# Recurrent attention with two expert layers on one core: attention's side steps reordered, GpSimd's queue in layer 1, unused products in the last chunks

## The chip, the cores and the metric

One core of one Trainium2 chip runs the kernel. The metric is the device time of one execution in microseconds; the kernel before was timed three times, and the median counts. The profile is of one further execution of the same program.

## The reference, cut to what matters

Three parts follow each other on 4 sequences of 768 tokens, with 8 heads of 48 channels:

```python
for t in range(768):                       # attention: a state of 48x48 per head
    cur = einsum('bhd,bhe->bhde', u * k_t, v_t)
    y_t = einsum('bhd,bhde->bhe', r_t, state + cur)
    state = w_t * state + einsum('bhd,bhe->bhde', k_t, v_t)
x = y reshaped to 3072 tokens x 384
...
e = argmax(x @ w_gate + modality_bias[modality_id])      # layer 1: one expert of 8 for a token
x = softmax weight * (relu(x @ w1[e]) @ w2[e])
...
top2 of x @ w_gate + log1p(exp(x @ w_noise)) * noise     # layer 2: two experts of 8 for a token
out = sum over the two: softmax weight * (relu(x @ w1[e]) @ w2[e])
```

The hidden width of an expert is 1024. Products of the expert layers are made as three f16 products (high times high, high times low, low times high), so each weight is converted into a high part by ScalarE and a low part by VectorE.

## The kernel before, in words

**Attention** (`attention`, L306) works in 24 chunks of 128 tokens, six to a sequence. The loop over `i` from -4 to 23 is a software pipeline whose order is written out by hand: in iteration `i` TensorE gets, in this order, `scores(i + 1)` (L422), `logits(i - 2)` (L221, the gate of layer 1), `outputs(i)` (`ps` L452, `py` L457 and L459), `turn(i - 1)` (L497), `keys_back(i + 1)` (L439) and the transposes of `k` and `r` of chunk `i + 3` and of `w` of chunk `i + 4` (L377). VectorE gets `products(i + 2)` (KT L402, RT L404), the two scans `decays_a` and `decays_b` (L386, L396), `diag` (L410), `state` (L469, L470) and `sums` (L479). ScalarE copies out of PSUM (`am` L427, `kt` L441, `xt` L499, `S` L476) and squares the rows (`norm`, L485). GpSimd masks `am` (L432) and makes `av` and `q` (L414, L369, L370).

At the end of an iteration stand the extra steps. `todo` holds those of layer 1's routing: after each sequence `route1a` in four steps `x` = 0 to 3 (logits out of PSUM, first maximum and exponential, `ranks` on TensorE at L250 to L254, row indices), one step an iteration, and `route1c`, which scatters the rows by index to the table R1 in DRAM (L537, on GpSimd's queue). `extra` holds what prepares the first visit of layer 1: the choice of its expert from counts (`first_a` to `first_d`, `counts` at L262), the gather of its weights (GW), the steps of their conversion (EC: `square` L794, `total` L207, `scales`, `split` with the high part at L812 and the low part at L815), the gather of its rows and their conversion (EX: L864, L226, L227, and a transposing DMA on SyncE's queue, L903). The constants FI, GW, N0, EC and EX say in which iteration each comes. A step that returns a function (the low part) has it called at once.

**Layer 1** makes seven visits of up to 448 rows of one expert (`Jobs.visit`, `Jobs.run`). A visit is eight blocks of the first product (L834, nine products each) and then the second product in columns (L849). Work for the neighbouring visits hangs in numbered slots, one after each block or half column: `turn_back` (L1112) and the gate of layer 2 for the visit before (L221), the fetch of the next visit's rows (`begin` at slot FE, its steps at slots XS), the scatter to table R2 of the visit two before (eight scatters, L1084, slots SCS), weights for later visits. The routing of layer 2 (`route2`, L1005) is a generator of some fifty VectorE steps, drawn four at a time by `tick` in the first eight slots; what is left is run at the end of the visit. Its last five operations are on GpSimd (L1076 to L1080), and with them ends what a scatter needs.

**Layer 2** runs 16 parts, eight experts with 512 and then 320 rows.

All DMAs of one queue start in the order of the program, and GpSimd's queue carries gathers, scatters and its own arithmetic in one order. The tiles of `pm` (logits, ranks, counts) share one PSUM bank.

Of the kernel before, what the change touches and what calls it, by code (L numbers as in the profile page):

```python
# [8 lines left out]
F32 = mybir.dt.float32  # L9
# [3 lines left out]
OP = mybir.AluOpType  # L13
# [5 lines left out]
P = 128  # L19
E = 8  # L20
# [3 lines left out]
NT = TOK // P  # L24
# [34 lines left out]
OE = 1  # L59
WI = -4  # L60
GI = (1, 2, 5, 8)
FI = 9
GW = (11, 12, 13, 16)
N0 = 15
EC = (15, 16, 17, 18, 18, 19, 20, 21, 22, 23, 23)
S1 = 3
EX = (19, 20, 20, 21, 21, 22)
FE = 1
CH = (6, 6, 6, 0)
TB = (0, 4)  # L70
LG = 2
XS = (1, 5, 6, 7, 8, 9)
XS1 = (5, 8, 9, 10, 11, 12)
SC1 = (0, 1, 1, 2, 3, 4, 5, 6)
SCS = (3, 4, 5, 6, 7, 8, 9, 10)
WS = (4, 5, 6, 7), (11, 12, 13, 14)


def bc(ap, shape):
    return ap.to_broadcast(shape)  # L80
# [3 lines left out]
def kernel(  # L84
# [163 lines left out]
    def ranks(x, m16, n, pr):  # L248

        nc.tensor.matmul(pr, tri, m16, start=True, stop=False)  # L250
        for c in range(n - 1):
            nc.tensor.matmul(pr[:, c + 1:, :], ones, bc(m16[:, c:c + 1, :], [P, n - 1 - c, E]),
                             start=False, stop=False)
        nc.tensor.matmul(pr, ones, bc(seen[x][:, None, :], [P, n, E]), start=False, stop=True)  # L254
        with nc.allow_low_precision(reason="counts up to 48 are exact"):
            sums = small.tile([P, E], F16, name="sums")
            nc.vector.tensor_reduce(sums, m16.rearrange("p c e -> p e c"), axis=AX, op=OP.add)
            nc.vector.tensor_tensor(seen[x], seen[x], sums, op=OP.add)
# [47 lines left out]
    def attention(extra):  # L306

        with ExitStack() as st:
# [173 lines left out]
            def norm(t):  # L482
                b, c = divmod(t, NC)
                sq = keep.tile([P, D], F16, name="sq")
                nc.scalar.activation(sq, row(t)[:, 0:META].bitcast(F32), AF.Square,  # L485
                                     accum_out=row(t)[:, META:ROW].bitcast(F32)[:, SS:SS + 1])
                if c == NC - 1:
                    meta = X[b % 2][:, :, META:ROW].bitcast(F32)
                    nc.gpsimd.tensor_copy(meta[:, :, 0], tok_all[:, b * NC:(b + 1) * NC])
                    nc.gpsimd.tensor_copy(meta[:, :, 2:2 + E], noise_sb[:, b * NC:(b + 1) * NC, :])  # L490

            def turn(t, pt=None):

                pt = ps_a.tile([P, HP, P], F32, name="pA") if pt is None else pt
                x = row(t)[:, 0:META].bitcast(F32)
                for i in range(NI):
                    nc.tensor.transpose(pt[:, i, :], x[:, i * P:(i + 1) * P], ident)  # L497
                XT[t] = keep.tile([P, NI, P], F32, name="xt", bufs=2)
                nc.scalar.copy(XT[t], pt[:, 0:NI, :])  # L499
# [7 lines left out]
            def route1a(b, x):  # L507

                sh = [P, NC, E]
                if x == 0:  # L510
                    R = RB[b] = {n: small.tile(s, d, name=f"r1{n}") for n, s, d in (
                        ("lg", sh, F32), ("ex", sh, F32), ("oh16", sh, F16), ("sm", [P, NC], F32),
                        ("ri", sh, F32), ("rf", [P, NC], F32), ("idx", [P, NC], I32))}
                    nc.vector.tensor_tensor(R["lg"], pl[b % 2], bias_all[:, b * NC:(b + 1) * NC, :], op=OP.add)
                    R["mx"], R["oh"], R["fm"] = first_max(R["lg"], NC, "r1")
                    R["fm"][0]()
                    return
                R = RB[b]
                if x == 1:
                    for f in R["fm"][1:]:  # L520
                        f()
                    nc.vector.tensor_tensor(R["lg"], R["lg"], bc(R["mx"][:, :, None], sh), op=OP.subtract)
                    nc.gpsimd.tensor_copy(R["oh16"], R["oh"])
                    nc.scalar.activation(R["ex"], R["lg"], AF.Exp)
                elif x == 2:
                    ranks(0, R["oh16"], NC, pr[b % 2])
                    nc.vector.tensor_reduce(R["sm"], R["ex"], axis=AX, op=OP.add)
                    nc.vector.tensor_scalar(R["sm"], R["sm"], 1e-9, None, op0=OP.add)
                    nc.vector.reciprocal(X[b % 2][:, :, META:ROW].bitcast(F32)[:, :, 1], R["sm"])
                else:  # L530
                    nc.vector.tensor_tensor(R["ri"], pr[b % 2], bc(erow[:, None, :], sh), op=OP.add)
                    nc.vector.tensor_tensor(R["ri"], R["ri"], R["oh"], op=OP.mult)
                    nc.vector.tensor_reduce(R["rf"], R["ri"], axis=AX, op=OP.add)
                    nc.vector.tensor_copy(R["idx"], R["rf"])
# [20 lines left out]
            for t in range(2, NL):  # L555
                load(t)

            def at(f, t):
                if 0 <= t < NT:
                    f(t)  # L560

            for i in range(-4, NT):
                for n, g in enumerate(data):
                    if i >= GI[n]:
                        next(g, None)
                if i >= 0:
                    at(scores, i + 1)
                at(norm, i - 1)
                at(products, i + 2)
                at(decays_a, i + 3)  # L570
                if i >= 0:
                    at(scores_out, i + 1)
                    at(masks, i + 1)
                at(logits, i - LG)
                at(decays_inv, i + 3)
                at(decays_b, i + 3)
                if i == -2:
                    scores(0)
                    scores_out(0)
                    masks(0)  # L580
                    if OE:
                        keys_back(0)
                o = {-1: 0, 0: -1}.get(i, i) if OE else i
                at(outputs, o)
                at(diag, i + 2)
                at(state, o)
                at(turn, i - 1)
                if i >= KB and (i >= 0 or not OE):
                    at(keys_back, i + 1)
                at(state_out, o)  # L590
                at(diag_v, i + 2)
                at(sums, o)
                for n, t in (("kr", i + 3), ("w", i + 4)):
                    at(lambda t: transposes(t, n), t)
                if 0 <= i < KB:
                    keys_back(i + 1)
                if i == WI:
                    warm(WARM[1])
                at(loads_q, i + 3)
                if i >= -2 and i + NL + 2 <= NT:  # L600
                    load(i + NL + 2)
                if i >= 0:
                    nc.sync.dma_start(out[i * P:(i + 1) * P, :], zt)
                for at_i, f, b, x in todo:
                    if at_i == i:
                        f(b, x)
                for f in extra.get(i, []):
                    f()

            last = {"rows": [lambda: norm(NT - 1)], "turn": lambda pt: turn(NT - 1, pt),  # L610
                    "logits": [lambda t=t: logits(t) for t in range(NT - LG, NT)],
                    "route": [], "scatter": []}
# [297 lines left out]
    class Jobs:  # L910
# [94 lines left out]
        def route2(self, xg, q, group="R2"):  # L1005
# [3 lines left out]
            t = lambda shape, n, dt=F32: vp.tile([P] + shape, dt, name=n)  # L1009
            R.row = X[q % 2][:, 0:NH, :]  # L1010
            R.inv = t([NH], "inv2")
            nc.gpsimd.memset(R.inv[VP // 32 * 32:P, :], 0.0)
            meta = xg[:, 0:NH, META:ROW].bitcast(F32)
            rm = R.row[:, :, META:ROW].bitcast(F32)

# [17 lines left out]
            def steps():  # L1033
# [39 lines left out]
                    yield dv.tensor_reduce(zi, z, axis=AX, op=OP.add)  # L1073
                for x in range(2):
                    yield dv.tensor_tensor(idx[:, x, :], zz[x][1], big, op=OP.add)
                nc.gpsimd.memset(rm, 0.0)  # L1076
                nc.gpsimd.tensor_copy(rm[:, :, 0], tok)
                nc.gpsimd.tensor_tensor(wa, o1, bc(d2[:, :, 0:1], sh), op=OP.mult)
                nc.gpsimd.tensor_tensor(tmp, o2, bc(d2[:, :, 1:2], sh), op=OP.mult)
                nc.gpsimd.tensor_tensor(rm[:, :, 1:1 + E], wa, tmp, op=OP.add)  # L1080
                R.idx = idx

            def scatter_one(h, x):
# [88 lines left out]
    def layers():  # L1172
# [5 lines left out]
        def add(hooks, s, f):  # L1178
            hooks.setdefault(s, []).append(f)
# [75 lines left out]
        def once(f):  # L1255
            f = f()
            if callable(f):
                f()

        def some(n):  # L1260
            for _ in range(n):
                once(steps0.pop(0))

        xsteps = []

        def begin(j, sidx):
# [6 lines left out]
                     (EC[0], lambda: steps0.extend(conv0()))):  # L1273
            add(extra, i, f)
        for i in EC:
            add(extra, i, lambda: some(1))
        for i in GW:
            add(extra, i, lambda: wsteps.pop(0)())
        for i in EX:
            add(extra, i, lambda: once(xsteps.pop(0)))  # L1280

        with tc.manual_schedule():
            last = attention(extra)
        with ExitStack() as st:
# [91 lines left out]
            with tc.manual_schedule():  # L1376
# [12 lines left out]
                for j in range(VISITS):  # L1389
                    hooks = {}  # L1390
                    q = max(0, j - EV + 1)
                    if j == 0:
# [11 lines left out]
                        add(hooks, S1 + 2, lambda: begin(1, early["sidx1"]))  # L1404
                        for s in XS1:
                            add(hooks, s, lambda: xsteps.pop(0)())
                        spread(hooks, steps0, (0, 1, 2, 3, 4, 5, 6))
                    else:
                        if j == 1:
                            for x, s in enumerate(T_PLAN):  # L1410
# [181 lines left out]
```

## Time and profile before

| | us |
|---|---|
| timed runs, median (lowest to highest) | 882.61 (881.57 to 887.2) |
| the profiled execution | 883.38 |
| span of its profile | 881.6 |
| TensorE busy in the span | 841.1 |
| mean granted TensorE clock | 0.954 of full |
| attention, up to the first block of layer 1 | about 211 |
| the seven visits of layer 1 | about 260 |

In the rows below a time is counted from the span's start. The chain of waits is followed back from the last instruction. A granted clock of 1.00 is TensorE's upper level (2.4 GHz) and 0.50 its lower one (1.2 GHz); figures between are a stretch with both.

### The profile page before, as it was taken

To read this page: it belongs to the slowest core of one execution; us is meant where nothing else is said; L and a number is where in the kernel's file an instruction comes from. 1 tells how busy PE (TensorE), PEld (TensorE's weight loads), DVE (VectorE), ACT (ScalarE), POOL (GpSimd) and SP (SyncE) were. 2 spreads that over 40 slices of the span, in tenths; PEclk is the share of its full clock that TensorE was granted. 3 is DMA by queue.
4 is the path that set the end of the run, shared out by engine and by line. 5 is a ranking of instruction groups with operands and counts; after the bars stand their busy time and mean duration, and the time that the engine had idled before them with its cause. 6 is when DMAs were issued, how large, how long until landed. Compare 5 with 4: busy or idle time off the path is not lost.

```text
span 881.6 us, 16060 instructions
## 1 busy us (share of the span) xinstructions
PE 841.1 (95%) x6161; PEld 633.1 (72%) x6161; DVE 464.3 (53%) x1244; ACT 435.0 (49%) x819; POOL 360.5 (41%) x404
## 2 busy tenths in 40 slices
PE   7999999989999989899999999999999999999993
PEld 6989999888576566565666678667686766768672
DVE  7979779873674466458666624333332423333220
ACT  2545346554354475567776426445444634534220
POOL 7957697942333161540424642232122223212222
PEclk9999799966999989999999999999999999999997
DMA  9986487423454231743574384864756546535231
GB/s 178 196 154 148 108 223 165 157 64 89 123 184 112 57 103 42 244 127 100 194 223 94 80 249 95 229 179 101 197 102 198 90 86 176 102 54 102 56 38 20
DMA packets 195077, 115.42 MB, mean 131 GB/s; under 512 B 173499, under 2 KB 183863, under 8 KB 193585
## 3 DMA queue, kind: packets, MB, share of 16 engines
q1 hardware_dynamic: 169088, 63.82, 29.6%
q0 software_dynamic: 18224, 50.12, 22.8%
q10 hardware_dynamic: 7680, 0.38, 0.6%
q8 instruction: 50, 0.82, 0.4%
q14 instruction: 35, 0.28, 0.1%
HBM read 73.37 MB, written 30.01 MB: 117 GB/s over the span
## 4 chain that ended last, share of the span: by engine, by line
PE 86%; DVE 4%; issue 3%; ACT 2%; POOL 1%; DMA 1%; ACTq 1%; POOLq 0%; DVEq 0%
PE ph L834 33%; PE po L841 20%; PE po L849 10%; PE py L459 4%; PE pm L221 4%; PE pA L422 3%; PE py L457 2%; PE po L858 2%; PE pTk L377 1%; PE pTr L377 1%; PE pTw L377 1%; PE pA L439 1%; PE po L1112 1%; PE pA L497 1%; PE ps L452 1%
## 5 line engine op out<-in xcount | busy, mean ns | idle before, releaser
L834 PE MATMUL ph<-xT,w1h 128*128 128x320 f16 (+2 forms) x1104 | 290.9, 350 | 3.4 <-DMA xT<-xs 1.5
L959 DVE SCALAR_TENSOR_TENSOR hl<-ph,hh 128x320 f16<-128x320 f32 (+2 forms) x184 | 110.0, 599 | 238.2 <-ACT hh L958 222.0
L1150 POOL DMA_INDIRECT out_dram<-y,oidx x56 | 87.6, 1563 | 268.0 <-ACT y L1149 265.6
L834 PE MATMUL ph<-xT,w1l 128*128 128x320 f16 (+2 forms) x552 | 192.0, 348 | 1.0 <-issue 1.0
L834 PEld LDWEIGHTS <-w1h 128*128 128x128 f16 x1104 | 155.1, 146 | 45.8 <-issue 9.9
L958 ACT ACTIVATE hh<-ph 128x320 f16<-128x320 f32 (+2 forms) x184 | 95.4, 521 | 124.8 <-PE ph L834 102.2
L841 PE MATMUL po<-w2h,hh 128*128 128x384 f16 x384 | 125.2, 326 | 0.5 <-issue 0.5
L841 PE MATMUL po<-w2l,hh 128*128 128x384 f16 x384 | 125.2, 326 | 0.0
L841 PE MATMUL po<-w2h,hl 128*128 128x384 f16 x384 | 125.2, 326 | 0.0
L841 PEld LDWEIGHTS <-hh 128*128 128x128 f16 x768 | 74.2, 98 | 48.4 <-issue 1.0
L834 PEld LDWEIGHTS <-w1l 128*128 128x128 f16 x552 | 79.7, 144 | 24.6 <-issue 3.9
L1149 ACT ACTIVATE y<-po,gf 128x384 f32<-128x384 f32 (+1 forms) x56 | 31.6, 577 | 113.7 <-PE po L841 83.4
L1084 POOL DMA_INDIRECT R<-X,idx x56 | 56.3, 1006 | 22.3 <-issue 13.3
L815 DVE SCALAR_TENSOR_TENSOR w1l<-stage,ps_w,w1h 128x1024 f16<-128x1024 f32 x36 | 47.7, 1340 | 25.8 <-ACT w1h L812 25.8
L849 PE MATMUL po<-hh,w2h 128*128 128x448 f16 x168 | 59.9, 356 | 1.1 <-issue 1.1
L849 PE MATMUL po<-hl,w2h 128*128 128x448 f16 x168 | 59.8, 356 | 0.7 <-issue 0.7
L849 PE MATMUL po<-hh,w2l 128*128 128x448 f16 x168 | 59.7, 355 | 0.7 <-issue 0.7
L459 PE MATMUL py<-vt,am 128*128 128x48 f32 x384 | 59.3, 286 | 0.0
L432 POOL TENSOR_SCALAR_AFFINE_SELECT am<-am 128x512 f32<-128x512 f32 x48 | 46.6, 992 | 30.8 <-ACT am L427 30.7
L849 PEld LDWEIGHTS <-w2h 128*128 128x128 f16 x336 | 33.1, 99 | 34.6 <-issue 5.3
L459 PEld LDWEIGHTS py<-vt,am 128*128 128x128 f32 x384 | 55.8, 212 | 0.2
L841 PEld LDWEIGHTS <-hl 128*128 128x128 f16 x384 | 37.6, 98 | 24.9
(323 smaller groups left out, 1410.8 us busy)
## 6 DMA issues: line engine op xcount, KB each, us to landing
stage<-in_moe_w_dram SPq DMA_DIRECT2D x16, 1536.0 KB
ldw<-in_w_dram SPq DMA_DIRECT2D x24, 192.0 KB
ldk<-in_k_dram SPq DMA_DIRECT2D x24, 192.0 KB
ldr<-in_r_dram SPq DMA_DIRECT2D x24, 192.0 KB
vt<-in_v_dram SPq DMA_DIRECT2D x24, 192.0 KB
out_dram<-zt SPq DMA_DIRECT2D x24, 192.0 KB
R<-X,idx POOLq DMA_INDIRECT x56
xT<-xg SPq DMA_TRANSPOSE x56
```

The costliest lines, as they stand in the source:

```text
L221: nc.tensor.matmul(pl, xT[:, i, :], g[:, i, :], start=i == 0, stop=i == NI - 1)
L432: nc.gpsimd.affine_select(m, m, pattern=[[0, HP], [1, P]], compare_op=OP.is_gt, fill=0.0, base=0, channel_multiplier=-1)
L459: nc.tensor.matmul(PY[t][:, hp, x], AM[t][x][:, hp, :], VT[t][:, 2 * hp + x], start=c == 0, stop=c == 0 or x == 1)
L815: nc.vector.scalar_tensor_tensor(l, v, s, h, op0=OP.mult, op1=OP.subtract)
L834: nc.tensor.matmul(ph, a[:, i, :].rearrange("p (q m) -> p m q", m=NM)[:, m, :], xT[:, b, cols], start=n == 0, stop=n == 3 * NI - 1)
L841: nc.tensor.matmul(py, a[m][:, cols], b[:, m, :], start=n == 0, stop=n == 3 * NM - 1)
L849: nc.tensor.matmul(py, b[:, m, d * P:(d + 1) * P], a[m][:, cols], start=n == 0, stop=n == 3 * NM - 1)
L958: nc.scalar.activation(hh[m][:, 0:T], ph, AF.Relu)
L959: nc.vector.scalar_tensor_tensor(hl[m][:, 0:T], ph, 0.0, hh[m][:, 0:T], op0=OP.max, op1=OP.subtract)
L1084: st = nc.gpsimd.indirect_dma_start(out=R2[:, :], out_offset=bass.IndirectOffsetOnAxis(ap=R.idx[0:VP, x, h:h + 1], axis=0), in_=R.row[0:VP ...
L1149: nc.scalar.activation(y[0:n], py[0:n], AF.Copy, scale=gf[0:n, h:h + 1])
L1150: st = nc.gpsimd.indirect_dma_start(out=out[:, :], out_offset=bass.IndirectOffsetOnAxis(ap=oidx[0:n, h:h + 1], axis=0), in_=y[0:n], in_off ...
```

## The change

It has four parts.

1. In attention the four steps of `route1a` are called before `outputs(i)` in place of the end of the iteration; the scatters `route1c` stay at the end. A function that an extra step returns (the low part of a weight or row conversion) is kept and called in the next iteration, just before the routing steps (`flush`). The exponential moves from `x` = 1 to 2, and what reads it from 2 to 3. The iterations of FI, GW and N0 move by one; EC makes nine conversion steps in attention in place of eleven, and `total` and `scales` of the second weight move into slots 0 and 1 of the first visit.
2. `keep_warm` puts products of a tile of ones, 512 columns each, whose result nobody reads, between the products of the last three chunks: two after `scores`, two after `logits`, two after `outputs`, and four more after the last `turn`; 22 in all.
3. In `route2` the memset of `R.inv` and the last operations move from GpSimd to VectorE, and the memset of the row's tail goes.
4. In layer 1 the fetch of the next visit's rows comes one slot earlier (FE, XS), the scatters from slot 1 on in place of 3 (SCS).

```diff
-FI = 9
-GW = (11, 12, 13, 16)
-N0 = 15
-EC = (15, 16, 17, 18, 18, 19, 20, 21, 22, 23, 23)
+FI = 10
+GW = (12, 13, 14, 17)
+N0 = 16
+EC = (16, 17, 18, 19, 20, 21, 22, 23, 23)
-FE = 1
+FE = 0
-XS = (1, 5, 6, 7, 8, 9)
+XS = (0, 4, 5, 6, 7, 8)
-SCS = (3, 4, 5, 6, 7, 8, 9, 10)
+SCS = (1, 2, 4, 5, 6, 8, 9, 10)
...
                     nc.gpsimd.tensor_copy(R["oh16"], R["oh"])
+                elif x == 2:
                     nc.scalar.activation(R["ex"], R["lg"], AF.Exp)
-                elif x == 2:
                     ranks(0, R["oh16"], NC, pr[b % 2])
+                else:
                     nc.vector.tensor_reduce(R["sm"], R["ex"], axis=AX, op=OP.add)
                     nc.vector.tensor_scalar(R["sm"], R["sm"], 1e-9, None, op0=OP.add)
                     nc.vector.reciprocal(X[b % 2][:, :, META:ROW].bitcast(F32)[:, :, 1], R["sm"])
-                else:
                     nc.vector.tensor_tensor(R["ri"], pr[b % 2], bc(erow[:, None, :], sh), op=OP.add)
...
+            def keep_warm(i, n):
+                if i >= NT - 3:
+                    t = ps_t.tile([P, HP, P], F32, name="pTw")
+                    for _ in range(n):
+                        nc.tensor.matmul(flat(t), ones, bc(ones[:, None, :], [P, HP, P]), start=True, stop=True)
...
+            second = []
+            def flush():
+                for f in second:
+                    f()
+                second.clear()
...
                     at(scores, i + 1)
+                    keep_warm(i, 2)
...
                 at(logits, i - LG)
+                keep_warm(i, 2)
                 at(decays_inv, i + 3)
                 at(decays_b, i + 3)
+                flush()
+                for at_i, f, b, x in todo:
+                    if at_i == i and f is route1a:
+                        f(b, x)
...
                 at(outputs, o)
+                keep_warm(i, 2)
                 at(diag, i + 2)
                 at(state, o)
                 at(turn, i - 1)
+                keep_warm(i, 4 * (i == NT - 1))
...
-                    if at_i == i:
+                    if at_i == i and f is route1c:
                         f(b, x)
                 for f in extra.get(i, []):
-                    f()
+                    f = f()
+                    if callable(f):
+                        second.append(f)
...
-            nc.gpsimd.memset(R.inv[VP // 32 * 32:P, :], 0.0)
+            nc.vector.memset(R.inv[VP // 32 * 32:P, :], 0.0)
...
-                nc.gpsimd.memset(rm, 0.0)
-                nc.gpsimd.tensor_copy(rm[:, :, 0], tok)
-                nc.gpsimd.tensor_tensor(wa, o1, bc(d2[:, :, 0:1], sh), op=OP.mult)
-                nc.gpsimd.tensor_tensor(tmp, o2, bc(d2[:, :, 1:2], sh), op=OP.mult)
-                nc.gpsimd.tensor_tensor(rm[:, :, 1:1 + E], wa, tmp, op=OP.add)
+                dv.tensor_tensor(wa, o1, bc(d2[:, :, 0:1], sh), op=OP.mult)
+                dv.tensor_tensor(tmp, o2, bc(d2[:, :, 1:2], sh), op=OP.mult)
+                yield
+                dv.tensor_tensor(rm[:, :, 1:1 + E], wa, tmp, op=OP.add)
+                dv.tensor_copy(rm[:, :, 0], tok)
...
-            add(extra, i, lambda: some(1))
+            add(extra, i, lambda: steps0.pop(0)())
...
-            add(extra, i, lambda: once(xsteps.pop(0)))
+            add(extra, i, lambda: xsteps.pop(0)())
...
-                        spread(hooks, steps0, (0, 1, 2, 3, 4, 5, 6))
+                        spread(hooks, steps0, (0, 1, 1, 2, 3, 4, 5))
```

## Rows read from the trace of the kernel before

**Rows 1.** Windows: busy us of PE, PEld, DVE, ACT, POOL; granted clock; DMA share; GB/s

```profile
160.00:180.00 20.00, 18.11 (x168) 17.31 (x168) 15.87 (x24) 10.38 (x22) 18.46 (x22) 0.84 0.23 80
180.00:200.00 20.00, 17.54 (x138) 16.41 (x137) 12.84 (x31) 10.32 (x22) 6.52 (x10) 0.67 0.26 67
200.00:220.00 20.00, 18.90 (x95) 15.87 (x95) 6.68 (x20) 9.03 (x18) 6.38 (x8) 0.65 0.26 90
```

**Rows 2.** Chain of waits, attention and first visits: start us, us, what

```profile
118.85 1.09 PE pA L422 x16
...
120.71 0.49 PE ps L452 x16
124.36 0.44 PE pA L439 x4
...
191.95 2.53 PE pA L422 x16
...
195.86 0.81 PE ps L452 x16
...
204.64 0.57 PE py L457 x2
...
209.83 0.67 PE pA L497 x3
...
211.06 3.21 PE ph L834 x9
...
214.60 1.70 PE ph L834 x9
...
240.73 2.40 DMA xT<-xs
...
288.70 0.52 issue
```

**Rows 3.** Waits of PE, 0 to 212 us: line waited for, us, times, longest

```profile
PE pA L497 <- ACT am L427: 4.4, 2, 2.5
...
PE pm L221 <- DVE r1lg L514: 1.9, 1, 1.9
...
PE pm L262 <- DVE seen L258: 1.3, 2, 0.8
...
PE pm L221 <- DVE r1rf L533: 0.6, 1, 0.6
PE ph L834 <- ACT xt L499: 0.5, 1, 0.5
```

**Rows 4.** Timeline of DVE and ACT, 163 to 206 us: start, us, engine, operation, idle before

```profile
164.91 2.85 DVE L815 SCALAR_TENSOR_TENSOR w1l<-stage,ps_w,w1h 128x1024 f16<-128x1024 f32 x1 [2.19 <-ACT w1h L812]
...
186.74 1.28 DVE L815 SCALAR_TENSOR_TENSOR w1l<-stage,ps_w,w1h 128x1024 f16<-128x1024 f32 x1 [1.35 <-ACT w1h L812]
...
192.98 1.48 ACT L794 ACTIVATE w2h<-stage 128x1536 f16<-128x1536 f32 x1
```

**Rows 5.** Timeline of POOL in the third visit: start, us, operation, idle before

```profile
275.86 0.24 POOL L1078 TENSOR_TENSOR wa<-oh_r2a,d 128x32 f32<-128x32 f32 x1 [14.93 <-DVE d L1067]
...
277.08 1.01 POOL L864 DMA_INDIRECT xg<-R,ev_sidx  x1 [0.16 <-issue]
278.40 0.98 POOL L1084 DMA_INDIRECT R<-X,idx  x1 [0.30 <-DVE pe_x L195]
...
287.73 0.94 POOL L1084 DMA_INDIRECT R<-X,idx  x1 [0.31 <-issue]
```

**Rows 6.** Waits of PE in layer 1, 212 to 480 us

```profile
PE pm L221 <- issue: 4.0, 7, 1.1
PE po L849 <- issue: 2.5, 7, 0.6
PE ph L834 <- issue: 2.4, 5, 1.0
PE ph L834 <- DMA xT<-xs: 1.5, 1, 1.5
```

More of the change, by code (lines that the diff above doesn't have):

```diff
@@ L604, in attention @@
                 for at_i, f, b, x in todo:
-                    if at_i == i:
+                    if at_i == i and f is route1c:
                         f(b, x)
                 for f in extra.get(i, []):
-                    f()
+                    f = f()
+                    if callable(f):
+                        second.append(f)
+            flush()
             last = {"rows": [lambda: norm(NT - 1)], "turn": lambda pt: turn(NT - 1, pt),
@@ L1258, in once @@
                 f()
-        def some(n):
-            for _ in range(n):
-                once(steps0.pop(0))
         xsteps = []
```

## The prediction, made before the changed kernel was run

> **What bounds the kernel now.** I read the windows first. From some 480 us on TensorE is busy all the time at the full clock, and the change touches nothing there but two scatters, so it has to pay in attention's last chunks or in layer 1. In 180 to 220 us TensorE is busy 36.4 of 40 us, and yet the granted clock is 0.67 and 0.65: the lower level for most of the stretch [rows 1]. The reader is to see that here a busy TensorE is a slow one. The chain of waits shows the price: from the start of `scores` to the end of `ps` a chunk takes 2.35 us at the full clock (118.85 to 121.20) and 4.72 at the lower (191.95 to 196.67); `outputs` with its `turn` takes 3.16 (121.20 to 124.36) against 5.86 (204.64 to 210.50); a first block of layer 1 takes 1.70 against 3.21 [rows 2]. The table of TensorE's waits then tells what stood before the fall: 2.5 us for ScalarE's copy `am`, and a chunk earlier 1.9 us for VectorE's reading of the logits out of the shared bank [rows 3]. The first of these two comes out of the extra steps: VectorE stands for a high part that ScalarE has yet to make (2.19 us, 1.35 us), all of VectorE's next chunk queues behind it, and ScalarE's next copies behind that [rows 4]. So the tail of attention is bound by TensorE at half clock, with waits made by the order of side steps. In layer 1 TensorE waits 10.4 us in all, 8.9 of them without a releaser that the profile shows [rows 6].
>
> **The change part by part.** The sum is made on the profiled execution, 883.38 us, which is 0.77 over the median of the timed runs.
>
> *Waits in attention.* With `route1a` ahead of `outputs`, VectorE reads the logits in the iteration that made them and no longer after `sums`, so the next iteration's `logits` find the bank free: -1.9. `counts` now come an iteration after `ranks`, so the two waits for `seen` go: -1.3. With the low parts deferred, VectorE meets a high part that is an iteration old, and ScalarE's `am` no longer waits behind a row conversion that waits for VectorE: -2.5 [rows 3]. Sum -5.7. What is late next is VectorE's `state`, which now has the routing steps ahead of it; see below. Bounds: 0 to -5.7. The cast of the first maximum moves ahead of `av` and `q` in GpSimd's queue and waits there for VectorE; both wait for VectorE's later `diag` anyway, so I cost it at nothing; should it hold them, the chunk is late by its wait, at most 0.5. The weight gathers and the choice of the expert come one chunk later, and the conversion with them; nothing waits for these before the first visit. The exponential's move puts it and its readers into one slot of the first visit; VectorE may wait there some 0.5 us for ScalarE, and four PSUM banks of blocks cover that.
>
> *The clock.* If the clock holds through the last two chunks, the three stretches above give -2.37, twice -2.70, and -1.51 for the first block: -9.3 [rows 2]. The rest of that half-clock stretch (a turn, keys, logits; some 3.4 us) gives about -1.5 at the same ratio of 1.85. Sum -10.8. Another 10 us of half clock lie at 159 to 163 and 176 to 183 (0.84 of the first window, the beginning of the second, [rows 1]), a loss of 4.5 by that ratio; no product stands there, but the wait of 1.9 us before the second goes. I take a third, -1.5. Bounds of the whole: 0 (the products don't hold it) to -15.3.
>
> *The products.* A 448-column product takes 1.70 / 9 = 0.189 us in a stream, so 512 columns take 0.216 and 22 of them 4.75 us; at the lower clock 3.21 / 9 gives 0.41 and 9.0 [rows 2]. They stand in TensorE's own stream and nothing else reads or waits for them. The waits of 0.6 and 0.5 us at the last logits and at the first block, for ScalarE's `xt` [rows 3], lie behind two and four of them and are filled: +4.75 - 1.1 = +3.65. The trace has no such product between others; bounds are 0 (all in waits) and 9.0, and I take the price of the stream since TensorE would be full.
>
> *New waits at the first visit.* The last row conversion's low part is deferred into the last chunk, and its transposing DMA on SyncE's queue with it (behind it there only the zeroing of `out`). ScalarE's part ends some 3 us into that chunk (my estimate: two copies, a high part and the row's own), VectorE needs two low parts (1.28 and about half of it for the narrower row), and the DMA 2.4 us [rows 2, 4]: about 7 us after the chunk's start, where TensorE is through in 6.2 (`logits` 0.77, ten products 2.2, `outputs` and `turn` 3.16). +0.5 for it. The two squares of the second weight (1.48 each [rows 4]) now both stand at the end of attention, and `total` in slot 0 of the first visit waits for them: TensorE, with the whole visit queued behind, stands about 0.6. Together +1.1; bounds 0 and 3. `scales` and the low parts follow two slots later than before; the second product that needs them is four slots further on.
>
> *VectorE behind.* VectorE is busy 15.9 of 20 us at 160 to 180 [rows 1], and in iteration 20 it gets two products, two scans, five routing steps, `state` and `sums`: 8 us or so (0.79 of a chunk of some 9 there, and the routing steps), where TensorE needs 6.8 (5.5 from 118.85 to 124.36, and three groups of transposes of 0.44 [rows 2]). I take +2 for its lag; bounds 0 and 4.7. The upper one: a low part took 2.85 us beside GpSimd's `av` and `q` and 1.28 with GpSimd idle [rows 4], and deferred ones fall beside GpSimd's masks: three times 1.57.
>
> The Trainium skill (GPSIMD Engine Reference, Key points) says that GpSimd shares its SBUF interfaces with VectorE, and that operations with two SBUF inputs contend. The two durations agree with it. By that rule each deferred part would cost the 2.85, which is the upper bound just given and gives the second rival its chance.
>
> *Layer 1.* GpSimd's queue stands 14.93 us at L1078 for VectorE; behind it are the gather of the next rows (277.08) and the eight scatters (278.40 to 287.73, one every 1.3 us) [rows 5]. With those operations on VectorE the gather can run during the visit before and the scatters start some 2 us earlier. Nobody waits for either: the fetched rows are needed a visit later, the scattered ones two layers of work later. TensorE's waits without a releaser begin where the scatters end (the last is issued at 287.73, the wait stands at 288.70 [rows 2, 5]), so they seem to hang on the scatters' number and spacing. Both stay, since the slots order the program but GpSimd runs ahead of them. I take 0. The four operations come to VectorE at the visits' seam, where the blocks' four PSUM banks cover them; if not, 4 x 0.24 us (GpSimd's own time for one, [rows 5]) x 6 visits = +5.8. At the other end, if the waits go with the queue's stall, -8.9 [rows 6]. The earlier slots of fetch and row conversion move work that is hidden behind the blocks; the wait of 1.5 us for the second visit's rows [rows 6] comes from the first visit, whose slots stay.
>
> Sum: -5.7 - 10.8 - 1.5 + 3.65 + 1.1 + 2 + 0 = -11.3. 883.38 - 11.3 = 872.1; against the median that is **871.3 us**.
>
> **The rivals.**
>
> *A, the products don't hold the clock (slower).* In 180 to 220 us TensorE was busy with short fp32 products and stayed at half [rows 1]; six products of 0.41 us in a chunk of over 11 us may not change that. For it: nothing in the trace shows such a mixture. Against it: the clock rose at once under the dense blocks at 211 (3.21 for the first, 1.70 for the next [rows 2]). Place: the last three chunks. It decides if the clock granted there is still near 0.5 though the waits are gone. Then -5.7 + 9.0 - 1.1 + 1.1 + 2 = +5.3: 887.9.
>
> *B, VectorE leads the tail.* The low parts at 2.85, the routing steps ahead of `state` and so of ScalarE's `S`, which `outputs` needs. For it: VectorE's share, and that the chain runs through the low parts. Against it: from iteration 21 on it has no scans. Place: iterations 20 to 22. About 5 of the gain go: 876.3.
>
> *C, the visits gain.* The freed queue takes the 8.9 us with it: 862.4. For it: they stand beside GpSimd's DMAs. Against it: these waits have no semaphore of GpSimd as releaser.
>
> *D, the move to VectorE costs at the seams*, or the change frees the queue in name only: +5.8, 877.1. For it: VectorE is the engine that `scatter` and the routing wait for. Against it: TensorE has no wait for VectorE in layer 1 [rows 6].
>
> **How the numbers follow.** Forecast 0.50 (866 to 877), A 0.10, B 0.18, C 0.12, D 0.10. The range 861 to 881 leaves out A, the upper ends of B and D and the lower end of C. About 1%, or 8.8 us, is what a measurement of this kernel can tell from no change: below 873.8 lie four fifths of the forecast, nearly all of C and a little of B and D, 0.55; above 891.4 only the far end of A, 0.04; between them 0.41.
>
> **What would show it.** Right: a granted clock near 1.0 from chunk 21 to the first visit; no wait of TensorE for `am`, `r1lg` or `seen` beyond the start; VectorE's low parts without a wait for ScalarE; the first block of layer 1 near 201 us (211.06 less 10.3, the sum up to there), at 1.7 us; waits without a releaser in layer 1 as long as before, some 2 us earlier. Wrong: half clock in the last chunks (A); TensorE waiting for `S`, KT or RT in chunks 20 to 23 (B); layer 1's seven visits shorter (C) or longer (D) than 260 us by over 5 us.

## The result and the profile after

The changed kernel took 873.81 us (median; 873.43 to 880.84) beside 882.61 for the kernel before on the same chip: a ratio of 0.9897, 95% interval 0.9859 to 0.9935. The forecast was 871.3, range 861 to 881. The execution whose profile follows is the slowest of the five (880.84), 7 us over the median. Beside the profile of before it loses 5 at the very start: scores of chunk 1 begin at 24.86 us instead of 19.98, after 11.8 us of half clock in the first chunk where before had 3.4. Nothing of the change is there, so places in the two profiles are compared from that point on. From it to the first block of layer 1 the time fell from 191.1 to 181.2 us; the prediction had -10.3. Runs of a kernel far above its fastest are left out of every ratio below; so on chip 3 below, where the kernel before itself spread from 857 to 880 us, the ratios stand nearer to 1 than the medians do.

The same three windows as [rows 1], of the changed kernel (columns as there):

```profile
160.00:180.00 20.00, 19.12 (x209) 18.04 (x209) 19.13 (x31) 9.53 (x22) 18.45 (x19) 1.00 0.35 128
180.00:200.00 20.00, 18.74 (x151) 15.38 (x149) 13.84 (x33) 11.24 (x24) 11.30 (x17) 0.83 0.37 97
200.00:220.00 20.00, 18.21 (x121) 14.19 (x121) 11.72 (x39) 12.26 (x24) 4.62 (x6) 1.00 0.21 72
```

The column to read is the granted clock (last but two): 0.84, 0.67, 0.65 became 1.00, 0.83, 1.00. TensorE's busy time is 56.1 us in the three windows where it was 54.6, and it does more of its work in it. VectorE is now at 19.13 of 20 us in the first window, from 15.87.

The waits of PE from 0 to 207 us, beside [rows 3]:

```profile
PE pA L422 <- DVE RT L404: 3.4, 1, 3.4
PE pm L250 <- POOL r1oh L523: 2.5, 2, 1.9
...
PE pA L497 <- ACT am L427: 1.5, 1, 1.5
PE ph L859 <- PE pTw L563: 1.2, 1, 1.2
PE pm L221 <- DVE pe_w L195: 0.8, 1, 0.8
...
PE pTw L563 <- PE pA L497: 0.6, 1, 0.6
```

The waits for `r1lg` and `seen` are gone. Of the two for `am` the one in chunk 22, 2.5 us, is gone; the 1.5 us left stand in chunk 6, where before had 1.9 and the change does nothing. The first line, 3.4 us, stands ahead of chunk 0 (2.4 in before). But the largest line behind it is new: the ranks wait for GpSimd's cast of the first maximum. GpSimd's timeline shows why:

```profile
131.90 1.06 POOL L786 DMA_INDIRECT stage<-in_moe_w_dram,ev_widx  x1 [0.30 <-issue]
132.97 1.23 POOL L432 TENSOR_SCALAR_AFFINE_SELECT am<-am 128x512 f32<-128x512 f32 x2
134.15 0.22 POOL L523 CAST r1oh<-oh_r 128x48 f16<-128x48 f32 x1
```

and TensorE's at the same time:

```profile
134.41 0.18 PE L250 MATMUL pm<-r1oh,tri 128*128 128x48 f16 x1 [1.91 <-POOL r1oh L523]
```

No idle time stands before the cast: GpSimd comes to it late, behind a gather and the masks, and the ranks, now ahead of `outputs`, take TensorE's whole queue along. 6.8 us of half clock follow in the clock's records. The products of no use, by line, all forms:

```profile
L563 PE MATMUL pTw<-ones x22: 376/379/634, 179.9 to 204.5; 128*128 128x512 f16 x22
```

379 ns is one from start to end; in a pair the second starts 0.22 us after the first, the price of the stream that the prediction took.

The low parts of the first weights on VectorE, beside [rows 4]:

```profile
193.01 1.28 DVE L840 SCALAR_TENSOR_TENSOR w1l<-stage,ps_w,w1h 128x1024 f16<-128x1024 f32 x1 [2.49 <-ACT w1h L837]
...
200.35 1.28 DVE L840 SCALAR_TENSOR_TENSOR w1l<-stage,ps_w,w1h 128x1024 f16<-128x1024 f32 x1 [2.29 <-ACT w1h L837]
```

They still wait for ScalarE, no shorter than before; but TensorE no longer has the wait for `am` behind them. The third visit in GpSimd's queue, beside [rows 5]:

```profile
256.31 1.31 POOL L889 DMA_INDIRECT xg<-R,ev_sidx  x1 [4.15 <-DVE nl L1074]
271.61 0.98 POOL L1109 DMA_INDIRECT R<-X,idx  x1 [13.99 <-ACT y L1131]
...
280.76 0.94 POOL L1109 DMA_INDIRECT R<-X,idx  x1 [0.30 <-issue]
```

The gather of the next rows went from 277.08 to 256.31, into the visit before, and the eight scatters still run 1.25 us apart. The waits of PE in layer 1, beside [rows 6]:

```profile
PE pm L221 <- issue: 7.8, 8, 1.5
PE ph L859 <- issue: 3.2, 7, 1.0
PE ph L859 <- DMA xT<-xs: 1.5, 1, 1.5
```

The waits without a releaser are 11.0 us (7.8 and 3.2) where 8.9 were. Counted from the first block of layer 1 to the first of layer 2, the seven visits take 242.3 us, from 240.2 (the "about 260" given for them ahead was too long).

### The profile page after: what moved, and what is told of

Its sections match the earlier page's. It is cut to its first block, busy times and chain, and to the rows that moved or that the text cites. A ratio compares the mean times of both kernels' runs of the same rounds, so it can differ in the third digit from the quotient of the medians.

```text
span 879.1 us, 16108 instructions
## 1 busy us (share of the span) xinstructions
PE 836.7 (95%) x6183; PEld 626.1 (71%) x6183; DVE 475.4 (54%) x1279; ACT 435.4 (50%) x819; POOL 351.3 (40%) x362
## 4 chain that ended last, share of the span: by engine, by line
PE 80%; POOL 7%; issue 5%; DVE 3%; ACT 2%; DMA 1%; ACTq 1%; POOLq 0%; SPq 0%; DVEq 0%
PE ph L859 33%; PE po L866 20%; PE po L874 10%; PE pm L221 3%; PE py L459 3%; PE po L883 2%; PE pA L422 2%; PE py L457 1%; POOL am L432 1%; POOL av L414 1%; PE po L1137 1%; POOL q L369 1%; POOL R L537 1%; PE pTw L377 1%; POOL q L370 1%
## 5 line engine op out<-in xcount | busy, mean ns | idle before, releaser
L859 PEld LDWEIGHTS <-w1h 128*128 128x128 f16 x1104 | 154.8, 146 | 49.6 <-issue 12.3
L840 DVE SCALAR_TENSOR_TENSOR w1l<-stage,ps_w,w1h 128x1024 f16<-128x1024 f32 x36 | 45.5, 1280 | 25.3 <-ACT w1h L837 25.3
L874 PEld LDWEIGHTS <-w2h 128*128 128x128 f16 x336 | 33.2, 99 | 31.0 <-issue 1.3
L432 POOL TENSOR_SCALAR_AFFINE_SELECT am<-am 128x512 f32<-128x512 f32 x48 | 43.5, 930 | 27.5 <-ACT am L427 27.3
```

The costliest lines, as they stand in the source:

```text
L432: nc.gpsimd.affine_select(m, m, pattern=[[0, HP], [1, P]], compare_op=OP.is_gt, fill=0.0, base=0, channel_multiplier=-1)
L840: nc.vector.scalar_tensor_tensor(l, v, s, h, op0=OP.mult, op1=OP.subtract)
L859: nc.tensor.matmul(ph, a[:, i, :].rearrange("p (q m) -> p m q", m=NM)[:, m, :], xT[:, b, cols], start=n == 0, stop=n == 3 * NI - 1)
L874: nc.tensor.matmul(py, b[:, m, d * P:(d + 1) * P], a[m][:, cols], start=n == 0, stop=n == 3 * NM - 1)
```

## The experiments

They ran on three chips, here 1, 2 and 3. The kernel before took 869.0 us on chip 1, 884.9 on chip 2 and 870.6 on chip 3. Where two changed kernels are compared, they are of one chip and the medians are given; a ratio is always to the kernel before on the same chip. A diff is to the changed kernel where nothing else is said.

**Chip 1. The products; layer 1's part; the cast.** The first kernel is the changed one, unaltered.

> The changed kernel once more, unaltered, as the measure for the three beside it: 873.8 us, within 1.5. If its profile shows 3 us of half clock at the start, where the profiled execution of before had 3.4 and that of after 13.7, the first block of layer 1 stands near 201 us; if it shows 13 us, near 206.

860.32 us, ratio 0.9907 (0.9875 to 0.9940). The 13.5 us under the expected time are the chip's: the kernel before is 13.7 us lower here too. The start had its 3.4 us of half clock, and the first block of layer 1 stood at 199.2 us. The start alone does not make the 206 of the first profile, though: on chip 3 the changed kernel had the slow start again (scores of chunk 1 at 24.91 us) and its first block at 201.3. From scores of chunk 1 to the first block the three profiles have 181.2, 179.3 and 176.4 us.

```diff
-                if i >= NT - 3:
+                if i >= NT:
```

> The changed kernel without the 22 products of no use. Theory (the products hold the clock in the last chunks): TensorE falls to the lower level from chunk 21 or 22 on as it did before, 9.3 us come back and 3.65 us of products go, so about +5.7: 879.5 us. Rival (the new order alone took the waits away and with them the fall of the clock): the clock holds without them and their price is saved, -3.65: 870.2 us.

870.03 us, ratio 1.0010 (0.9969 to 1.0051): the whole gain is gone, 9.7 us over the kernel with products. Windows of this kernel:

```profile
180.00:200.00 20.00, 18.17 (x108) 16.73 (x107) 12.24 (x27) 10.83 (x24) 10.85 (x11) 0.60 0.36 109
200.00:220.00 20.00, 19.43 (x112) 14.16 (x111) 12.61 (x45) 12.09 (x21) 1.50 (x3) 0.89 0.10 33
```

and of the one with them, on the same chip:

```profile
180.00:200.00 20.00, 18.59 (x172) 15.22 (x169) 11.93 (x28) 12.07 (x25) 11.17 (x12) 1.00 0.44 124
200.00:220.00 20.00, 20.00 (x122) 14.32 (x121) 14.28 (x51) 10.41 (x21) 2.13 (x3) 1.00 0.13 45
```

Busy time is about the same, the clock 0.60 against 1.00. In this pair the products hold it and the new order alone does not. The attention of the two profiles differs little all the same: from scores of chunk 1 to the first block 181.0 us without products and 179.3 with them, since the kernel with them had more half clock ahead of the tail (17.1 us from scores of chunk 10 to the first block, all before chunk 23, beside 10.2 there without).

```diff
-FE = 0
-XS = (0, 4, 5, 6, 7, 8)
-SCS = (1, 2, 4, 5, 6, 8, 9, 10)
+FE = 1
+XS = (1, 5, 6, 7, 8, 9)
+SCS = (3, 4, 5, 6, 7, 8, 9, 10)
...
-                dv.tensor_tensor(wa, o1, bc(d2[:, :, 0:1], sh), op=OP.mult)
-                dv.tensor_tensor(tmp, o2, bc(d2[:, :, 1:2], sh), op=OP.mult)
-                yield
-                dv.tensor_tensor(rm[:, :, 1:1 + E], wa, tmp, op=OP.add)
-                dv.tensor_copy(rm[:, :, 0], tok)
+                nc.gpsimd.memset(rm, 0.0)
+                nc.gpsimd.tensor_copy(rm[:, :, 0], tok)
+                nc.gpsimd.tensor_tensor(wa, o1, bc(d2[:, :, 0:1], sh), op=OP.mult)
...
```

> Attention's part and the products stay; what the change did to layer 1's visits is undone (memsets, the row's weights and the token's number again on GpSimd, the former slots of fetch, conversion and scatters). Theory (layer 1's part is worth nothing, GpSimd's queue stands either way and its scatters set the waits): the same within 1.5 us, 873.8, and layer 1's seven visits within 2 us of the 242.3 of the changed kernel. Rival C (the freed queue gains in the visits): 3 to 8.9 us longer, 877 to 883. Rival D (the work costs at VectorE): up to 5.8 us shorter, 868.

857.29 us, ratio 0.9848 (0.9798 to 0.9897), 3.0 us under the changed kernel; the visits took 221.1 us against 230.1. Its profile also shows the products failing once:

```profile
180.00:200.00 20.00, 20.00 (x99) 16.00 (x100) 10.35 (x24) 9.87 (x22) 8.35 (x9) 0.50 0.36 88
```

After a wait of 0.55 us for the cast at 176.83 the clock fell at 179.7 and stayed at the lower level for 30.7 us, products and all, with TensorE busy 20.00 of 20.00. This is the prediction's rival A, in one execution.

```diff
-                    nc.gpsimd.tensor_copy(R["oh16"], R["oh"])
+                    nc.vector.tensor_copy(R["oh16"], R["oh"])
```

> One line: the cast of the first maximum to fp16 is made by VectorE, which has just written it, instead of GpSimd, whose queue runs late. Theory (the cast in GpSimd's queue makes TensorE's ranks wait 1.9 and 0.6 us, and the clock falls behind these waits for 6.8 us twice): no wait of ranks for GpSimd, both low stretches gone, -2.5 and about -6.2 (13.6 us of half clock at the ratio of 1.85), 865 us. Rival (TensorE's waits only move to another releaser, since GpSimd is late anyway with av, q and the masks): 873.8 within 1.5 us.

859.51 us, ratio 0.9891 (0.9839 to 0.9944): the same. No ranks waited for GpSimd, but `py` now waited 0.6 us for GpSimd's mask and the logits 0.8 us for VectorE, and 6.8 us of half clock followed each of these two. The changed kernel beside it waited 0.3 us for the cast in its profile, not 2.5. My theory fell: a stretch of half clock is not priced by the wait that one sees ahead of it in one execution.

**Chip 2. Each part on the kernel before.** The first two diffs are to the kernel before.

> The kernel before once more, unaltered, for a second profile of it beside the three others: a ratio of 1.00 within 0.004. If the profile shows layer 1's seven visits at 240 us with waits without a releaser of 9 us or so, as the first profile of before did, these waits are a habit of the kernel; if it shows them near the 221 us of the kernel with attention's part alone, they are a matter of the execution.

883.64 us, ratio 1.0013 (0.9979 to 1.0047). The visits took 240.6 us, and TensorE's waits between 200 and 455 us are those of [rows 6] again:

```profile
PE ph L834 <- issue: 3.1, 6, 1.0
PE pm L221 <- issue: 3.0, 5, 1.8
PE po L849 <- issue: 2.8, 6, 1.0
PE ph L834 <- DMA xT<-xs: 1.6, 1, 1.6
```

In the first comparison and on this chip, where the kernel before takes 883 and 885 us, all six profiles have waits of TensorE without a releaser in layer 1; in the eight profiles of chips 1 and 3, where it takes 869 and 871, there are none. They go with the chip more than with the kernel. That they make up much of those 14 us is my inference; the kernel before was not profiled on chips 1 and 3.

```diff
-FE = 1
-XS = (1, 5, 6, 7, 8, 9)
-SCS = (3, 4, 5, 6, 7, 8, 9, 10)
+FE = 0
+XS = (0, 4, 5, 6, 7, 8)
+SCS = (1, 2, 4, 5, 6, 8, 9, 10)
...
+                dv.tensor_tensor(wa, o1, bc(d2[:, :, 0:1], sh), op=OP.mult)
...
```

> The kernel before with layer 1's part of the change alone: the four operations and the memset on VectorE, fetch, row conversion and scatters in their new slots. Theory (the earlier slots put the next rows' conversion among VectorE's low parts of the weights at the visits' seam, ScalarE waits for it, its squares are late and TensorE waits for these, as 3.4 us in the fourth visit of the second profile of the changed kernel): +3 us, a ratio of 1.003 to 1.007. The prediction's value: 0, 1.000. Rival C: 0.990 to 0.997.

887.98 us, ratio 1.0071 (1.0033 to 1.0109), 3.1 us over the kernel before by the medians; visits 244.5 us. Layer 1's part alone costs. It does not cost by the wait that was expected: between 200 and 455 us TensorE waits for no square (`w2h`) here, and the two largest lines are

```profile
PE pm L221 <- issue: 7.2, 11, 1.7
PE ph L834 <- issue: 3.5, 7, 1.0
```

10.7 us without a releaser in place of the 8.9 above. What made them longer was not found.

```diff
+                if i >= NT - 3:
+                    t = ps_t.tile([P, HP, P], F32, name="pTw")
+                    for _ in range(n):
+                        nc.tensor.matmul(flat(t), ones, bc(ones[:, None, :], [P, HP, P]), start=True, stop=True)
...
+                    keep_warm(i, 2)
...
```

> The kernel before with the 22 products alone. Theory (the products, not the new order, hold the clock in the tail; without them the changed kernel was at 1.001): a ratio near 0.990, the last chunk at the full clock. Rival (the waits of 2.5 and 1.9 us that the old order leaves let the clock fall all the same, and the products then cost 9.0): 1.003 to 1.006, the last chunk at half clock.

882.43 us, ratio 1.0006 (0.9971 to 1.0041): not told apart from nothing, and neither of the two values expected. The mechanism was there, with no half clock from scores of chunk 23 to layer 1 and 14.85 us for that stretch against 19.18 in the kernel before on that chip. But the old order's waits and falls in chunks 14, 17 and 21 stayed (some 29 us of half clock), and the 4.75 us of products are paid.

```diff
-FE = 0
-XS = (0, 4, 5, 6, 7, 8)
-SCS = (1, 2, 4, 5, 6, 8, 9, 10)
+FE = 1
+XS = (1, 5, 6, 7, 8, 9)
+SCS = (3, 4, 5, 6, 7, 8, 9, 10)
```

> The changed kernel with the former slots of fetch, row conversion and scatters in layer 1, but the four operations and the memset on VectorE as in the change. Theory (the slots cost, the operations don't): as with attention's part alone, a ratio near 0.985, and layer 1's seven visits near 221 us. Rival D (the operations at the seams cost): as the changed kernel, 0.990, visits near 230 us.

875.65 us, ratio 0.9905 (0.9868 to 0.9943), visits 240.0 us. By the ratio it is the changed kernel; by its visits it is the kernel before (240.6), 4.5 us under the one with the new slots too (244.5). Neither the changed kernel nor attention's part alone ran on this chip, so this run doesn't part operations from slots. The theory's ratio, 0.985, lies outside its interval; rival D's, 0.990, within.

**Chip 3. The layer's part again, the order alone, the scatters apart.**

> The changed kernel unaltered, beside the three others: a ratio of 0.990 within 0.004, as twice before.

857.69 us, ratio 0.9936 (0.9883 to 0.9990).

> Attention's part and the products, layer 1 as in the kernel before; the second measurement of it. Theory (layer 1's part costs 3 to 6 us, as 1.0071 for that part alone says): 0.983 to 0.987, faster than the changed kernel beside it by 0.4 to 0.7%. Rival (the first measurement lay low by chance, the part is worth 0 as predicted): 0.990.

851.94 us, ratio 0.9883 (0.9781 to 0.9985), 5.8 us under the changed kernel; visits 219.8 us against 230.4. The kernels differ as on chip 1. Waits of PE, 200 to 455 us, in the changed kernel:

```profile
PE ph L859 <- DMA xT<-xs: 7.0, 3, 4.0
PE po L207 <- ACT w2h L819: 3.4, 2, 2.1
```

and in attention's part alone:

```profile
PE ph L859 <- DMA xT<-xs: 1.5, 1, 1.5
PE po L874 <- DVE hl L984: 0.2, 1, 0.2
```

(In the second kernel the wait of 1.5 us before the first block lies ahead of 200 us and is not counted.) The fourth, fifth and sixth visit take 36.8, 35.5 and 33.2 us in the changed kernel, 31.7, 31.5 and 31.7 in attention's part alone: all of the 10.6 us. The place of the 3.4 us is in the fourth visit. The timeline of the changed kernel there (start, us, engine, operation, idle before):

```profile
307.98 3.68 DVE L840 SCALAR_TENSOR_TENSOR w1l<-stage,ps_w,w1h 128x1024 f16<-128x1024 f32 x3
...
312.32 0.17 DVE L198 TENSOR_SCALAR ps_g<-pe_g 128x4 int32<-128x4 int32 x1
...
312.52 0.61 ACT L226 ACTIVATE xs<-xg,ps_g 112x384 f16<-112x384 f32 x1 [3.45 <-DVE ps_g L198]
...
313.05 1.47 ACT L819 ACTIVATE w2h<-stage 128x1536 f16<-128x1536 f32 x1
...
314.65 0.16 PE L207 MATMUL po<-wssq,ones_b 128*128 128x1 bf16 x1 [2.12 <-ACT w2h L819]
```

and of attention's part alone:

```profile
304.97 3.67 DVE L840 SCALAR_TENSOR_TENSOR w1l<-stage,ps_w,w1h 128x1024 f16<-128x1024 f32 x3
...
305.96 1.47 ACT L819 ACTIVATE w2h<-stage 128x1536 f16<-128x1536 f32 x1
...
310.54 0.61 ACT L226 ACTIVATE xs<-xg,ps_g 112x384 f16<-112x384 f32 x1 [1.12 <-DVE ps_g L198]
```

Read them by the order in ScalarE's queue. With slot 0 in XS the conversion of the next rows stands ahead of the squares of the second weight; it waits 3.45 us for a scale that VectorE makes behind three low parts; so the squares start 5 us after the low parts did in place of 1, and `total` waits for them on TensorE with the visit's blocks behind it. The four profiles with the new slots on chips 1 and 3 all have this wait; the four with the old slots have none. The wait of 4.0 us for `xT` is another matter: it stands where the sixth visit begins, and the kernel of the next experiment has it, 5.3 us long, with the former slots. So about half of the 10.6 us, the fourth visit's, is traced to the slot; the cause of the other half is not shown.

```diff
-                if i >= NT - 3:
+                if i >= NT:
```

> Attention's new order alone: no products of no use, layer 1 as in the kernel before. Theory (the terms add: order without products and with layer 1's part is 1.001, layer 1's part is +0.3 to +0.7%): 0.994 to 0.998, the last chunk at half clock. The prediction's own terms for the order alone, -5.7 + 1.1 + 2 = -2.6: 0.997. Rival (order and products gain only together, and the order alone gives nothing): 1.001.

(The diff is to attention's part alone.) 863.25 us, ratio 1.0001 (0.9941 to 1.0060): the rival's value, though the interval holds the prediction's 0.997. Beside the same kernel with products it is 11.3 us slower. Its profiled execution (857.95 us, the fastest of its twelve; 848.58 in the kernel with products) does not have the difference in attention:

```profile
180.00:200.00 20.00, 18.47 (x148) 16.20 (x144) 12.39 (x28) 12.62 (x28) 10.53 (x12) 0.80 0.35 106
200.00:220.00 20.00, 20.00 (x116) 14.17 (x115) 13.72 (x50) 9.92 (x19) 2.20 (x3) 0.95 0.18 63
```

```profile
PE ph L859 <- DMA xT<-xs: 6.8, 2, 5.3
```

From scores of chunk 1 to the first block it took 176.9 us, with products 178.1. The visits took 228.9 against 219.8 us, with the same code: 2.0 of these lie in the first visit, where half clock ran on, and 7.1 in the fifth and sixth, around the 5.3 us for `xT`. What the order alone gives isn't settled: nothing by the ratio, -7.3 us by the two medians, and by difference on chip 1 (no products, 870.03; less 3.0 for layer 1's part; 868.95 before) -1.9.

```diff
             def scatter_one(h, x):
+                if self.mark is not None:
+                    m1 = small.tile([P, NC], F32, name="r1sm")
+                    nc.gpsimd.tensor_copy(m1[:, 0:1], self.mark[:, 0:1])
...
-                hh[m] = self.vp.tile([P, SA], F16, name="hh", bufs=10)
+                hh[m] = self.mark = self.vp.tile([P, SA], F16, name="hh", bufs=10)
...
```

> Attention's part and the products as in the kernel beside it, and each of layer 1's scatters behind a small copy on GpSimd that reads the newest hidden or output column, so that the scatters keep to their slots, 2 us and more apart, instead of running 1.25 us apart. Theory (TensorE's waits without a releaser hang on series of eight transfers from GpSimd's queue close together): on a chip where the kernel before has these waits, most of the 9 us of them and the half clock behind them go, 0.970 to 0.978. Rival (they hang on something else, such as the number of transfers): as attention's part alone, 0.985, or up to 0.5% over it for the copies' waits.

849.29 us, ratio 0.9833 (0.9768 to 0.9899), the fastest of all. Most of the scatters moved apart:

```profile
300.76 0.95 POOL L1117 DMA_INDIRECT R<-X,idx  x1 [0.63 <-DVE pi_w L199]
...
305.86 0.95 POOL L1117 DMA_INDIRECT R<-X,idx  x1 [0.62 <-DVE hl L985]
```

where the kernel beside it has

```profile
295.73 0.94 POOL L1109 DMA_INDIRECT R<-X,idx  x1 [0.30 <-DVE pe_x L195]
296.97 0.94 POOL L1109 DMA_INDIRECT R<-X,idx  x1 [0.30 <-DVE hl L984]
```

But this chip shows no waits without a releaser in any kernel, so the question that the run was made for stays open, and 2.65 us under attention's part alone is within the two kernels' intervals. By the medians, attention's part without layer 1's, spaced or not, beats both kernels on the chips on which it ran.

## Why the prediction came out right

The time and the sign held, and attention's last chunks left the half clock, as forecast. Less of the rest was right than the total says. Point by point.

**Clock, -12.3: the tail rose, and the time needs the products; where their gain lies is not shown.** The half clock from scores of chunk 23 to the first block, from the clock's records:

```
without products: before 19.2, 19.2; no products 18.0; layer 1 only 6.4; order only 6.2 us
with products:    changed 0.05, 0, 0; cast 0; products only 0; operations only 0;
                  attention's part 24.5, 0; spaced 0 us
```

Eight of nine have next to none with products, none of five without. Taken together with their price, products are worth 9.7 us (chip 1) and 11.3 (chip 3) in the new order, where -12.3 + 3.65 = -8.65 was forecast. That it is the clock, the timed runs show as well: over all runs of a kernel the mean granted clock is 0.977 with products and 0.963 without on chip 1, 0.980 and 0.964 on chip 3. That is 25 and 30 us of half clock less in a run; at 0.46, the share that is lost at the ratio of 1.85, it gives 11 and 14 us, and 7 and 9 after the price of 4.75.

But the tail does not hold that much. With 6.2 us of half clock the stretch from scores of chunk 23 to the first block took 14.2 us in order alone; with products it took 14.5 to 15.5 in those eight, because their price is paid there. All of attention, from scores of chunk 1, took 181.0 and 176.9 us in the new order without products, 176.4 to 181.2 with them (188.6 in the one where they failed). In the profiled pairs much of the products' gain lies in layer 1's visits: 3.5 of 6.6 us on chip 1, 9.1 of 9.4 on chip 3. How products in attention's last chunks would act on the fifth visit was not found.

The sum also added order and products as two independent terms. By the ratios they gain only together: products in the old order 1.0006, the new order without products 1.0010 (with layer 1's part) and 1.0001, the two together 0.985 and 0.988. Why, and what the order alone is worth, stays open. Rival A is real but rare.

**Products, +3.65: the price right.** The 0.22 us of one in a stream was measured, 22 of them. Of the 1.1 us of waits that they were to fill, the first profile has 0.6 ahead of a product.

**Waits in attention, -5.7: these went, but a new one came.** The waits for `r1lg`, for `seen` and for `am` in chunk 22 are gone in the first profile, all 5.7 us. The failed step is the sentence on GpSimd's cast, "I cost it at nothing ... at most 0.5": I looked at what the cast could hold up behind itself on GpSimd, not at who reads it and how late GpSimd's queue runs (18.46 of 20 us busy in [rows 1]). The ranks waited 1.9 and 0.6 us, which leaves -3.2. The later profiles of the changed kernel have 0.3 us and none of this wait (and 2.0 and 0.5 us of new waits behind VectorE's work on the counts), and the cast on VectorE gained nothing in time; so 2.5 us is the size in one execution. "VectorE meets a high part that is an iteration old" was wrong too: it stands 2.49 us, where [rows 4] had 2.19.

**New waits, +1.1: the size right, the split not.** The first block waits 1.2 us (1.1 and 1.5 in the later profiles, for the DMA of `xT`), where 0.5 was forecast; `total` in the first visit, forecast at 0.6, didn't wait. **VectorE behind, +2: about 1**, with 0.8 for `pe_w` and 0.4 for `S`.

**Layer 1, 0: wrong.** Medians on one chip put its part at +3.0, +3.1 and +5.8 us. The step that failed: "The earlier slots of fetch and row conversion move work that is hidden behind the blocks". The gain of the rows' earlier arrival is nothing, as said; but on chips 1 and 3 the earlier conversion passed the squares in ScalarE's queue, which TensorE waits for, 3.4 us. Rival D had the size (+5.8) and put it on the four operations; on these chips the traces put about half of it on a slot. On chip 2 the part cost without that wait, and no run parts operations from slots on one chip, so the operations are not cleared. That GpSimd's free queue brings nothing (rival C) stood: with the operations on VectorE and the former slots the visits took 240.0 us, 240.6 in the kernel before, in one profile each.

What paid for the cast's wait in the first comparison was the clock ahead of the tail, where only a third of 4.5 us had been reckoned. From scores of chunk 1 to the first block the records hold 48.4 us of half clock in the profile of before and 18.9 in that of the changed kernel: 29.5 us less, at 0.46 a gain of 13.6 us, where the sum had 10.8 up to that block. So -9.9 beside the forecast of -10.3 is in part luck: two misses of 2.5 and 2.8 us cancel.

## What to carry to other kernels

Before a step is moved to an earlier slot, write down each queue that it enters and what it passes there: a wait of 3.4 us came here from a small operation that waits, put ahead of one that the bottleneck needs. A cast on an engine that is 92% busy is as late as that queue, not as short as the cast. And where TensorE is busy and yet at half clock, a few dense products between may return twice their price on top of it; try them with the waits taken out and with the waits left in, since here they gained in the new order alone, and take several profiles, since one in nine says the contrary.

## What the runs showed that I had not expected

The same wait, quite different prices. In eight profiles TensorE waits 0.94 or 0.95 us in chunk 14; the half clock in that chunk is 0, 0, 0, 3.4, 3.4, 6.4, 9.6 and 9.6 us. So what one execution loses behind a wait is no measure of the wait.

A TensorE without any idle time can stay at the lower level, 0.50 for 20.00 busy us of 20.00 (the window above). The Trainium skill (TensorE: Matmul & The Clock Gate, Part 1) says that the lower clock is the default state and that activity releases it. By the busy column this window does not agree: 20.00 us busy, and no release.

The waits without a releaser in layer 1, 9 to 11 us in a profile, are there or not there by the chip, and a kernel's time differs by 14 us between chips whose runs agree among themselves. What these waits are was not found. The wait of 2.4 to 5.3 us for `xT` at the sixth visit is open too: five of the eight profiles of chips 1 and 3 have it, one of them with the former slots.
